# Output projection of an attention branch: plain fp32 operands in place of split halves, and a row broadcast written by ten copies in place of three

## The chip, the cores and the metric

The kernel runs on one core of a Trainium2 chip. The metric is the device time of one execution in microseconds (us). TensorE (PE in the profile) multiplies matrices, VectorE (DVE), ScalarE (ACT) and GpSimd (POOL) work elementwise, and SyncE (SP) issues nearly all transfers; these are carried by the core's 16 DMA engines. Each engine takes its instructions in the order in which they stand in its queue.

## The reference

Sequence length S = 2048, width D = 576, 32 heads of 18, a gate branch of width 2304. Cut to what matters:

```python
x = A_x
xn = layernorm(x)
qkv = (xn @ wqkv)                    # 32 heads, 18 wide
p = softmax(q k^T * 18**-0.5, masked to the last 256 positions)
s = (p @ v).reshape(1, S, D) @ wo    # the output projection
z1, z2 = split(gelu(xn @ w_in))      # 2304 each
g = silu((z1 * (w_sp @ layernorm(z2) + b_sp)) @ w_out)
return x + s * g
```

Everything is float32. The change concerns `s`: the division by the softmax's sums and the product with `wo`.

## The kernel before

**Precision by halves.** Most products are made from split operands. `split` (L117) writes a high part of a float32 tile in the type fp32r (a copy on ACT) and the rest, source minus high part, as a low part (a subtraction on DVE). A product is then three matmuls: high by high, high by low, low by high. Two places use plain fp32 operands: the products of probabilities with values (`pv`, L552, whose tiles `pt` and `vg` are fp32) and the transposes (L309). By its loops, `pv` issues 256 matmuls with 384 streamed columns, 224 with 256 and 224 with 128; four heads stand side by side in column groups of 32, so four such matmuls go together.

**The stages that the change touches.** They are the last three.

1. *The product stage* (L991 on) multiplies `w_sp` with the normed z2 by a Strassen scheme: three groups g of seven products n, with eight steps s each, so 168 steps m. One step is 18 matmuls (L1001) of 512 columns. For step m, `load_w` (L220, the DMA is on L224) brings the tile `spr` of 128 by 1024 four steps ahead into one of three buffers, so the load issued at step m waits for the split of the data of step m+1; `split_step` splits the data of step m+2 into `sph` (ACT, 1024 wide) and `spl` (DVE), both on L229. In the last group, idle room is used for what comes later. `pump` (L179) starts units from a list as credit allows and forms them two steps later; `later(k, ...)` (L917) puts a job k steps ahead.
2. *Units for the output projection.* `sums_unit` (L874), listed at step 124, loads the softmax's sums, inverts them, stores them as `r_d` (32 heads by 2048), and four steps later spreads them to `re_d`, one row for every row of the attention's output, by three copies from DRAM to DRAM: all 32 heads (576 rows), then two for the 64 rows that the layout repeats (10 rows of one head, 54 rows of three heads). A row is 2048 floats, 8,192 bytes. `weight_unit` (L854) loads and splits a block of `wo` or `w_out`, `o_unit` (L862) loads and divides the first two chunks of the output (`wo_load` L815, `wo_split` L826). `free_tile` (L896) reuses tiles of the products as they end: two tiles for the halves of `wo` (`wow`), four for ten blocks of `w_out` (`wos`).
3. *The bridge* (L1074 on) does the output projection for eight chunks t of 256 positions, two blocks of 128 each. A block is 14 pairs of stationary and streamed operand, each in two halves of 288 columns: 28 matmuls (L1100, `wops`). Beside them the next chunk is loaded, multiplied with the inverted sums and split, and four blocks of `w_out` and the first chunk of y are prepared. Its result goes through `so` (ACT L1114) to `s_d`.
4. *The end stage* multiplies y with `w_out`: 1728 matmuls of 288 columns (L1143, `po`), with the last four blocks of `w_out` loaded at its start.

The order of the queues is the program's own order there (a manual schedule for PE, ACT, DVE, POOL and SP in the product stage and the bridge, for PE in the end stage).

Of the kernel before, what the change touches and what calls it, by code (L numbers as in the profile page):

```python
# [9 lines left out]
F32 = mybir.dt.float32  # L10
F32R = mybir.dt.float32r
AF = mybir.ActivationFunctionType
ALU = mybir.AluOpType
# [45 lines left out]
def f32(ap):  # L59
    return ap.bitcast(F32)  # L60
# [3 lines left out]
def kernel(  # L64
# [52 lines left out]
    def split(hi, lo, src):  # L117
        act.activation(hi, src, AF.Copy)
        dve.tensor_tensor(lo, src, f32(hi), ALU.subtract)
# [695 lines left out]
    def wo_load(to, t, rooms):  # L815
        ts_ = slice(t * 2 * P, (t + 1) * 2 * P)
        raw = to.tile([P, 5, 2 * P], F32, name="oraw", bufs=1)
        rs = rooms()
        n = 5 // len(rs) + 1 if len(rs) > 1 else 5
        sp.dma_start(raw, o_d[:, ts_].rearrange("(k p) c -> p k c", p=P))  # L820
        for i, ap in enumerate(rs):
            kz = min(i * n + n, 5)
            sp.dma_start(ap[:, :kz - i * n], re_d[i * n * P:kz * P, ts_].rearrange("(k p) c -> p k c", p=P))
        return raw, rs

    def wo_split(ohl, got):  # L826
        raw, rs = got
        oh, ol = ohl[:, 0:5], ohl[:, 5:9]
        for n in range(3):
            ks = slice(2 * n, min(2 * n + 2, 5))  # L830
            rr = rs[0][:, ks] if len(rs) == 1 else rs[n][:, :ks.stop - ks.start]
            dve.tensor_tensor(raw[:, ks], raw[:, ks], rr, ALU.mult)
            act.activation(oh[:, ks], raw[:, ks], AF.Copy)
            if n < 2:
                dve.tensor_tensor(ol[:, ks], raw[:, ks], f32(oh[:, ks]), ALU.subtract)
            else:
                dve.tensor_tensor(oh[64:128, 4], raw[64:128, 4], f32(oh[64:128, 4]), ALU.subtract)
        return oh, ol

    wow, wos, parts, ohls = [], {}, [], {}  # L840

    with ExitStack() as ph:
        wk = open_pool(ph, "wk", bufs=2)
# [7 lines left out]
        OPENS = (0, 2, 4, 6)  # L851
        due, now = {}, 0

        def weight_unit(src, h, l):  # L854
            def load():
                raw = wk.tile([P, D], F32, name="zr", bufs=ZRB)
                sp.dma_start(raw, src)
                return raw

            return load, lambda raw: split(h, l, raw), 1  # L860

        def o_unit(t):  # L862
            def rooms():
                return [wk.tile([P, D], F32, name="zr", bufs=ZRB)[:, :512].rearrange("p (k c) -> p k c", k=2)
                        for _ in range(3)]

            def form(got):
                ohl = (pre.tile([P, 8 * ZW], F32R, name="z0")[:, :18 * P].rearrange("p (k c) -> p k c", k=9) if t else
                       ow.tile([P, 9, 2 * P], F32R, name="ohl", bufs=1))
                ohls[t] = wo_split(ohl, got)  # L870

            return lambda: wo_load(ow, t, rooms), form, 3

        def sums_unit():  # L874

            flat = [t.rearrange("h (a c) -> (h a) c", c=512) for t in (d_d, r_d)]

            def load():
                raw = wk.tile([P, D], F32, name="zr", bufs=ZRB)[:, :512]
                sp.dma_start(raw, flat[0])  # L880
                return raw

            def form(raw):
                dve.reciprocal(raw, raw)
                sp.dma_start(flat[1], raw)
                h, d = divmod(512, DH)
                for to, src in ((re_d[:D].rearrange("(h d) s -> h d s", d=DH),
                                 r_d.unsqueeze(1).to_broadcast([H, DH, S])),
                                (re_d[D:D + DH - d], r_d[h].unsqueeze(0).to_broadcast([DH - d, S])),
                                (re_d[D + DH - d:].rearrange("(h d) s -> h d s", d=DH),  # L890
                                 r_d[h + 1:].unsqueeze(1).to_broadcast([H - h - 1, DH, S]))):
                    later(4, sp.dma_start, to, src)

            return load, form, 1

        def free_tile(n):  # L896

            pool_, name = homes[PRODUCTS[n][1]]
            t = pool_.tile([P, 8 * ZW], F32R, name=name)
            made = [t[:, i * D:(i + 1) * D] for i in range(5)]  # L900
            if n < 3:
                wow.append(made)
                if n == 2:
                    return [weight_unit(wo[:, k, :], wow[0][k], wow[1][k]) for k in range(5)]
                return []
            parts.extend(made)
            us = [o_unit(n - 4)] if n in (4, 5) else []
            while len(parts) > 1:
                f = len(wos)
                wos[f] = parts.pop(0), parts.pop(0)  # L910
                us.append(weight_unit(w_out[f * P:(f + 1) * P, :], *wos[f]))
            return us
# [4 lines left out]
        def later(k, fn, *args):  # L917
            due.setdefault(now + k, []).append(partial(fn, *args))
# [109 lines left out]
    with ExitStack() as ph:  # L1028
# [22 lines left out]
        def wout_unit(to, f):  # L1051
            def load():
                raw = yp.tile([P, D], F32, name="wr")
                sp.dma_start(raw, w_out[f * P:(f + 1) * P, :])
                return raw

            def form(raw):
                split(*to, raw)
                wos[f] = to

            return load, form
# [12 lines left out]
        with ExitStack() as bridge:  # L1074
            zp = open_pool(bridge, "zp", bufs=2, side="right")
            wps = open_pool(bridge, "wps", bufs=2, space=PSUM)
            wl4 = yp.tile([P, 8 * D], F32R, name="wl4", bufs=1)

            def rooms():
                return [zp.tile([P, 5, 2 * P], F32, name="rraw")]  # L1080

            nxt = []
            ws = [wout_unit([wl4[:, (2 * n + a) * D:(2 * n + a + 1) * D] for a in range(2)], 10 + n) for n in range(4)]
            yu = [y_unit(0, k, nxt) for k in range(NF // 3)]
            plan = [ws[:2], ws[2:]] + [[y] for y in yu]
            oraws, got, outs = {}, [], []
            for t in range(NS // 2):
                if t + 2 < NS // 2:
                    oraws[t + 2] = wo_load((ow, zp)[t % 2], t + 2, rooms)
                oh, ol = ohls.pop(t)  # L1090
                for c in range(2):
                    cs = slice(c * P, (c + 1) * P)
                    po = wps.tile([P, 2, 512], F32, name="wops")
                    pl = []
                    for k in range(4):
                        pl += [(oh[:, k], wow[0][k]), (oh[:, k], wow[1][k]), (ol[:, k], wow[0][k])]
                    pl += [(oh[:, 4], wow[0][4]), (oh[:, 4], wow[1][4])]
                    for n, (lt, r) in enumerate(pl):
                        for i in range(2):
                            pe.matmul(po[:, i, :288], lt[:, cs], r[:, i * 288:(i + 1) * 288], start=n == 0,  # L1100
                                      stop=n == len(pl) - 1)
                    if c == 0:
                        if t and t + 1 < NS // 2:
                            to = (ow, zp)[(t + 1) % 2]
                            ohls[t + 1] = wo_split(to.tile([P, 9, 2 * P], F32R, name="ohl", bufs=1), oraws.pop(t + 1))
                    else:
                        while got:
                            form, raw = got.pop(0)
                            form(raw)
                        got = [(form, load()) for load, form in plan[t]]  # L1110
                    if outs:
                        sp.dma_start(*outs.pop(0))
                    so = zp.tile([P, D], F32, name="so")
                    act.activation(so.rearrange("p (a b) -> p a b", a=2), po[:, :, :288], AF.Copy)  # L1114
                    rows = slice(t * 2 * P + c * P, t * 2 * P + (c + 1) * P)
                    outs.append((s_d[rows, :], so))
            sp.dma_start(*outs.pop(0))
            while got:
                form, raw = got.pop(0)
                form(raw)  # L1120
# [3 lines left out]
        ph.enter_context(tc.manual_schedule(engines={ET.PE}))  # L1124
        outp = open_pool(ph, "outp", bufs=2, space=PSUM)
        fin = open_pool(ph, "fin", bufs=2)
        wow = [xp.tile([P, 8 * ZW], F32R, name=homes[PRODUCTS[n][1]][1]) for n in (1, 2)]
        more = [w[:, i * D:(i + 1) * D] for w in wow for i in range(4)]
        for f in range(14, NF):
            load_wout(more[2 * (f - 14):2 * (f - 14) + 2], f)  # L1130
        CH = list(range(8))
        for n, tc_ in enumerate(CH):
            ys = nxt
# [82 lines left out]
```

## Time and profile before

| what | value |
|---|---|
| median of 3 runs | 1939.07 us (1938.62 to 1939.74) |
| the profiled execution's own time | 1937.71 us |
| its span in the profile | 1936.0 us |
| PE busy | 1910.9 us, 99% of the span |
| DVE, ACT, POOL busy | 1076.2, 892.4, 288.1 us |
| matmuls of the output projection (L1100) | 448 |
| matmuls of the end stage (L1143) | 1728 |

The profile is one execution. A group's row names line, engine, operation, written and read tiles, shapes and count, then busy time, mean time of one, and idle time of the engine before them with what ended it. The chain of waits follows the work that ended last back to what released it. A row of a stage table gives for a stretch of time the busy time of each engine with its count, the granted PE clock, the mean busy share of the 16 DMA engines, and the GB/s that they moved. A matmul's recorded length includes its way through the array, so that records overlap: what one costs in a run is the distance from start to start.

### The profile page before, as it was taken

The numbers are of one execution on the slowest core, as the hardware profiler recorded it, in microseconds if no ns is written. First come the engines' busy times: TensorE is split into PE (matmuls) and PEld (weight loads), VectorE is DVE, ScalarE is ACT, GpSimd is POOL, SyncE is SP. The second block draws the span as 40 slices with busy tenths as digits, with TensorE's granted clock in tenths as the row PEclk, the third lists the DMA queues.
The fourth block names the chain that finished last, engine by engine and source line by source line (L and its number), as shares of the span: only waits on it lengthen the run. The fifth ranks groups of instructions, "written<-read, shape, count | busy, mean of one in ns | idle before, by whom it ended". The sixth has DMA issues, their size and how long they took to land.

```text
span 1936.0 us, 30625 instructions
## 1 busy us (share of the span) xinstructions
PE 1910.9 (99%) x11095; PEld 1658.4 (86%) x11095; DVE 1076.2 (56%) x2294; ACT 892.4 (46%) x1663; POOL 288.1 (15%) x388
## 2 busy tenths in 40 slices
PE   7999999999999999999999999999999999999998
PEld 5889999998777787877788888888888878999998
DVE  6522243367666666663277777666776877533322
ACT  4212222216665666666575566545655345422211
POOL 1101243433332333333100000000000000000000
PEclk9999999999999999999999999999999999999999
DMA  7655578975554655544576687757867778954442
GB/s 218 193 136 164 193 256 274 286 239 137 133 145 117 151 140 135 132 132 130 181 252 212 208 269 243 236 165 235 280 217 238 236 243 279 304 182 145 147 139 66
DMA packets 218510, 376.88 MB, mean 195 GB/s; under 512 B 40383, under 2 KB 117055, under 8 KB 217591
## 3 DMA queue, kind: packets, MB, share of 16 engines
q1 hardware_dynamic: 214135, 367.75, 61.9%
q10 hardware_dynamic: 2304, 5.09, 0.7%
q0 software_dynamic: 1920, 2.09, 0.4%
q8 instruction: 87, 1.43, 0.3%
q14 instruction: 64, 0.52, 0.1%
HBM read 261.76 MB, written 117.81 MB: 196 GB/s over the span
## 4 chain that ended last, share of the span: by engine, by line
PE 95%; DMA 3%; DVE 1%; ACT 1%; issue 0%; SPq 0%; DVEq 0%; ACTq 0%
PE acc L1001 34%; PE mm L460 12%; PE mm L688 12%; PE po L1143 12%; PE mm L326 6%; PE tps L539 5%; PE sp L409 5%; PE ops L562 4%; PE vps L478 3%; PE wops L1100 2%; DMA s_d<-so 1%; DMA spr<-sc_d 1%; DMA wraw<-in_wqkv_dram 1%; PE tpt L309 0%; DMA xr<-in_x_dram 0%
## 5 line engine op out<-in xcount | busy, mean ns | idle before, releaser
L1001 PE MATMUL acc<-sph,zh 128*128 128x512 f32 x1008 | 392.8, 390 | 3.8 <-ACT sph L229 3.7
L1001 PE MATMUL acc<-spl,zh 128*128 128x512 f32 x1008 | 393.0, 390 | 0.8 <-DVE spl L229 0.8
L1001 PE MATMUL acc<-sph,zl 128*128 128x512 f32 x1008 | 392.7, 390 | 0.0
L413 DVE CUSTOM_DVE_ANT_0 junk<-sp,band 128x384 bf16<-128x384 f32 (+1 forms) x512 | 273.7, 540 | 142.8 <-PE sp L409 138.6
L543 ACT ACTIVATE pt<-tps 128x384 f32<-128x384 f32 (+2 forms) x576 | 247.9, 439 | 125.4 <-PE tps L539 115.8
L460 PE MATMUL mm<-b,z1wh 128*128 128x512 f32 x648 | 250.2, 398 | 0.0
L229 DVE TENSOR_TENSOR spl<-spr,sph 128x1024 fp32r<-128x1024 f32 x166 | 203.2, 1224 | 65.7 <-ACT sph L229 64.8
L1001 PEld LDWEIGHTS acc<-sph,zh 128*128 128x128 f32 x1008 | 189.5, 188 | 44.1 <-ACT sph L229 4.1
L1001 PEld LDWEIGHTS acc<-spl,zh 128*128 128x128 f32 x1008 | 189.6, 188 | 40.7 <-DVE spl L229 1.1
L1001 PEld LDWEIGHTS acc<-sph,zl 128*128 128x128 f32 x1008 | 189.6, 188 | 39.2
L688 PE MATMUL mm<-z2wh,b 128*128 128x384 f32 x720 | 193.1, 335 | 0.0
L539 PE MATMUL tps<-att 128*128 128x384 f32 (+1 forms) x576 | 188.1, 327 | 0.9 <-ACT pt L543 0.8
L229 ACT ACTIVATE zh<-b 128x384 fp32r<-128x384 f32 x144 | 75.8, 527 | 241.2 <-PE acc L1001 241.1
L229 ACT ACTIVATE sph<-spr 128x1024 fp32r<-128x1024 f32 x166 | 174.2, 1049 | 20.2 <-DMA spr<-sc_d 10.4
L409 PE MATMUL sp<-att 118*128 118x384 f32 (+1 forms) x512 | 171.9, 336 | 0.0
L1143 PE MATMUL po<-b,yh 128*128 128x288 f32 x896 | 155.8, 296 | 0.0
L229 DVE TENSOR_TENSOR zl<-b,zh 128x384 fp32r<-128x384 f32 x144 | 80.1, 556 | 114.0 <-ACT zh L229 113.9
L460 PE MATMUL mm<-b,z1wl 128*128 128x512 f32 x360 | 142.7, 396 | 0.0
L460 PEld LDWEIGHTS mm<-b,z1wh 128*128 128x128 f32 x648 | 122.2, 189 | 23.9 <-issue 4.9
L688 PE MATMUL mm<-z2wl,b 128*128 128x384 f32 x400 | 134.0, 335 | 0.0
L539 PEld LDWEIGHTS tps<-att 128*128 128x128 f32 x576 | 109.1, 189 | 26.7 <-issue 7.6
L1143 PEld LDWEIGHTS po<-b,yh 128*128 128x128 f32 x896 | 131.9, 189 | 0.0
(159 smaller groups left out, 2793.9 us busy)
## 6 DMA issues: line engine op xcount, KB each, us to landing
spr<-sc_d SPq DMA_DIRECT2D x96, 512.0 KB
spr<-in_w_sp_dram SPq DMA_DIRECT2D x72, 512.0 KB
zr<-z_d SPq DMA_DIRECT2D x136, 192.0 KB
st_d<-qkhl SPq DMA_DIRECT2D x72, 256.0 KB
z_d<-zt SPq DMA_DIRECT2D x96, 192.0 KB
z_d<-z1o SPq DMA_DIRECT2D x72, 256.0 KB
z1t<-z_d SPq DMA_DIRECT2D x72, 256.0 KB
yr<-y_d SPq DMA_DIRECT2D x48, 384.0 KB
```

The source lines that it names most:

```text
L229: job()
L326: pe.matmul(ps, w, r, start=n == 0, stop=n == len(pl) - 1)
L409: pe.matmul(ps[:, :w], q_of(u, j)[:DR, i * P:(i + 1) * P], k_of(u, j)[:DR, k0:k0 + w], start=True, stop=True)
L413: dve.tensor_tensor_reduce(out=junk[:, :w], in0=ps[:, :w], in1=band[:, m0:m0 + w], scale=1.0, scalar=-3.0e38, op0=ALU.add, op1=ALU.max, ac ...
L460: pe.matmul(ps, w, r, start=n == 0, stop=n == len(pl) - 1)
L478: pe.matmul(ps[:, i, :288], r, w[:, i * 288:(i + 1) * 288], start=n == 0, stop=n == len(pl) - 1)
L539: pe.matmul(ps[:, :m * P], k_of(u, j)[:, (kb - base) * P:(kb - base + 1) * P], q_of(u, j)[:, (a - lo) * P:(a - lo + m) * P], start=True, s ...
L543: act.activation(pt[:, j, d0:d0 + n * P], ps[:, (qa - a) * P:(qa - a + n) * P], AF.Exp, scale=scale)
L562: pe.matmul(o_ps[c][32 * j:32 * j + 32, (lo - 4 * c) * P:(hi - 4 * c + 1) * P], vgs[u][:, kb - k0, j * VW:j * VW + 32], pt[:, j, (lo - kb) ...
L688: pe.matmul(ps[:, :ZW], r, wt, start=n == 0, stop=n == len(pl) - 1)
L1001: pe.matmul(acc[j], z[:, ps], w[:, cs], start=s == i == 0 and n in OPENS, stop=s == 7 and i == 2, skip_group_check=True)
L1143: pe.matmul(po[i][:, a, :288], y[:, i * P:(i + 1) * P], w[:, a * 288:(a + 1) * 288], start=f == 0 and m == 0, stop=f == NF - 1 and m == 2)
```

## The change

In words: `wo` is copied to one fp32 tile (ACT), not split. The divided output `o` is one fp32 tile, written by the DVE multiplication directly; its split (three copies on ACT, three subtractions on DVE a chunk) is gone. A block is five matmuls for each half of 288 columns, plain fp32, the fifth on 64 rows: 10 instead of 28. Only one product tile is needed for `wo`, so five tiles hold twelve blocks of `w_out`; the bridge then prepares blocks 12 to 15 and the end stage two instead of four. The spread of the inverted sums is ten copies, eight of four heads (72 rows) and the two for the repeated rows, two in a step over five steps.

```diff
-    def wo_split(ohl, got):
+    def wo_divide(o, got):
...
-            dve.tensor_tensor(raw[:, ks], raw[:, ks], rr, ALU.mult)
-            act.activation(oh[:, ks], raw[:, ks], AF.Copy)
...
+            dve.tensor_tensor(o[:, ks], raw[:, ks], rr, ALU.mult)
+        return o
...
-            return load, lambda raw: split(h, l, raw), 1
+            return load, lambda raw: split(h, l, raw) if l is not None else act.activation(h, raw, AF.Copy), 1
...
-                for to, src in ((re_d[:D].rearrange("(h d) s -> h d s", d=DH),
-                                 r_d.unsqueeze(1).to_broadcast([H, DH, S])),
-                                (re_d[D:D + DH - d], r_d[h].unsqueeze(0).to_broadcast([DH - d, S])),
-                                (re_d[D + DH - d:].rearrange("(h d) s -> h d s", d=DH),
-                                 r_d[h + 1:].unsqueeze(1).to_broadcast([H - h - 1, DH, S]))):
-                    later(4, sp.dma_start, to, src)
+                spread = [(re_d[h0 * DH:(h0 + 4) * DH].rearrange("(h d) s -> h d s", d=DH),
+                           r_d[h0:h0 + 4].unsqueeze(1).to_broadcast([4, DH, S])) for h0 in range(0, H, 4)]
+                spread += [(re_d[D:D + DH - d], r_d[h].unsqueeze(0).to_broadcast([DH - d, S])),
+                           (re_d[D + DH - d:].rearrange("(h d) s -> h d s", d=DH),
+                            r_d[h + 1:].unsqueeze(1).to_broadcast([H - h - 1, DH, S]))]
+                for n, (to, src) in enumerate(spread):
+                    later(4 + n // 2, lambda to=to, src=src: spreads.append(sp.dma_start(to, src)))
...
-                    pl = []
-                    for k in range(4):
-                        pl += [(oh[:, k], wow[0][k]), (oh[:, k], wow[1][k]), (ol[:, k], wow[0][k])]
-                    pl += [(oh[:, 4], wow[0][4]), (oh[:, 4], wow[1][4])]
-                    for n, (lt, r) in enumerate(pl):
+                    for k in range(5):
+                        kp = slice(0, P if k < 4 else 64)
                         for i in range(2):
-                            pe.matmul(po[:, i, :288], lt[:, cs], r[:, i * 288:(i + 1) * 288], start=n == 0,
-                                      stop=n == len(pl) - 1)
+                            pe.matmul(po[:, i, :288], o[kp, k, cs], wow[k][kp, i * 288:(i + 1) * 288], start=k == 0,
+                                      stop=k == 4)
```

How the queues stand, at the two places that matter most. First SP's queue in the last group of the product stage, where the inverted sums are spread (`re_d<-r_d`) between the loads of the product's tiles (`spr<-sc_d`), of blocks of `w_out` (`zr<-in_w_out_dram`) and of z1 (`z1t`). Before:

```order
L885 DMA r_d<-zr 128x512
L224 DMA spr<-sc_d 128x1024 x3
L857 DMA zr<-in_w_out_dram 128x576 x2
L224 DMA spr<-sc_d 128x1024
L1013 DMA re_d<-r_d 576x1x2048
L1013 DMA re_d<-r_d 10x2048
L1013 DMA re_d<-r_d 54x1x2048
L224 DMA spr<-sc_d 128x1024 x4
L929 DMA z1t<-z_d 128x512 x2
```

The same place of SP's queue in the change, from the load ahead of the first copy to the load behind the last:

```order
L224 DMA spr<-sc_d 128x1024
L852 DMA zr<-in_w_out_dram 128x576
L892 DMA re_d<-r_d 72x1x2048 x2
L224 DMA spr<-sc_d 128x1024
L852 DMA zr<-in_w_out_dram 128x576
L892 DMA re_d<-r_d 72x1x2048 x2
L224 DMA spr<-sc_d 128x1024
L892 DMA re_d<-r_d 72x1x2048 x2
L224 DMA spr<-sc_d 128x1024
L892 DMA re_d<-r_d 72x1x2048 x2
L224 DMA spr<-sc_d 128x1024
L892 DMA re_d<-r_d 10x2048
```

Behind these rows stand the copy of 54 rows, two loads of `z1t` and the next load of `spr`. The copies begin behind the same load as before, and each following load of `spr` now stands behind two more of them.

Second, PE's queue where the product stage ends and the bridge begins. Before, with the two halves of `wo` in turn (`b_15839`, `b_15840`) against the halves of the divided output (`ohl`):

```order
L1001 MATMUL acc_16766<-sph,zl 128x512
L1100 MATMUL wops<-b_15839,ohl 128x288 x2
L1100 MATMUL wops<-b_15840,ohl 128x288 x2
L1100 MATMUL wops<-b_15839,ohl 128x288 x4
L1100 MATMUL wops<-b_15840,ohl 128x288 x2
```

In the change, the whole bridge and the first matmuls of the end stage (`z_16801` is the divided output of the second chunk):

```order
L999 MATMUL acc_16770<-sph,zl 128x512
L1095 MATMUL wops<-b_15839,o 128x288 x20
L1095 MATMUL wops<-b_15839,z_16801 128x288 x20
L1095 MATMUL wops<-b_15839,o 128x288 x120
L1138 MATMUL po_17449<-b_15840,yh 128x288 x4
L1138 MATMUL po_17449<-b_15840,yl 128x288 x2
```

The bridge stands at the same place of PE's queue, with 160 matmuls where 448 were.

More of the change, by code (lines that the diff above doesn't have):

```diff
@@ L824, in wo_load @@
         return raw, rs
-    def wo_split(ohl, got):
+    def wo_divide(o, got):
         raw, rs = got
-        oh, ol = ohl[:, 0:5], ohl[:, 5:9]
         for n in range(3):
@@ L831, in wo_split @@
             rr = rs[0][:, ks] if len(rs) == 1 else rs[n][:, :ks.stop - ks.start]
-            dve.tensor_tensor(raw[:, ks], raw[:, ks], rr, ALU.mult)
-            act.activation(oh[:, ks], raw[:, ks], AF.Copy)
[L834 to L840, printed above, removed]
+            dve.tensor_tensor(o[:, ks], raw[:, ks], rr, ALU.mult)
+        return o
+    spreads = []
+    wow, wos, parts, divided = [], {}, [], {}
     with ExitStack() as ph:
@@ L852, with weight_unit @@
         due, now = {}, 0
-        def weight_unit(src, h, l):
+        def weight_unit(src, h, l=None):
             def load():
@@ L867, in form, with load @@
             def form(got):
[L868 to L872, printed above, removed]
+                o = (pre.tile([P, 8 * ZW], F32, name="z0")[:, :10 * P].rearrange("p (k c) -> p k c", k=5) if t else
+                     ow.tile([P, 5, 2 * P], F32, name="o", bufs=1))
+                divided[t] = wo_divide(o, got)
+            def load():
+                assert len(spreads) == 10
+                return wo_load(ow, t, rooms)
+            return load, form, 3
         def sums_unit():
@@ L898, in free_tile @@
             pool_, name = homes[PRODUCTS[n][1]]
-            t = pool_.tile([P, 8 * ZW], F32R, name=name)
+            t = pool_.tile([P, 8 * ZW], F32 if n == 1 else F32R, name=name)
             made = [t[:, i * D:(i + 1) * D] for i in range(5)]
[L901 to L905, printed above, removed]
+            if n == 1:
+                wow.extend(made)
+                return [weight_unit(wo[:, k, :], wow[k]) for k in range(5)]
             parts.extend(made)
@@ L1082 @@
             nxt = []
-            ws = [wout_unit([wl4[:, (2 * n + a) * D:(2 * n + a + 1) * D] for a in range(2)], 10 + n) for n in range(4)]
+            ws = [wout_unit([wl4[:, (2 * n + a) * D:(2 * n + a + 1) * D] for a in range(2)], 12 + n) for n in range(4)]
             yu = [y_unit(0, k, nxt) for k in range(NF // 3)]
@@ L1089 @@
                     oraws[t + 2] = wo_load((ow, zp)[t % 2], t + 2, rooms)
-                oh, ol = ohls.pop(t)
+                o = divided.pop(t)
                 for c in range(2):
@@ L1104 @@
                             to = (ow, zp)[(t + 1) % 2]
-                            ohls[t + 1] = wo_split(to.tile([P, 9, 2 * P], F32R, name="ohl", bufs=1), oraws.pop(t + 1))
+                            divided[t + 1] = wo_divide(to.tile([P, 5, 2 * P], F32, name="o", bufs=1), oraws.pop(t + 1))
                     else:
@@ L1126 @@
         fin = open_pool(ph, "fin", bufs=2)
-        wow = [xp.tile([P, 8 * ZW], F32R, name=homes[PRODUCTS[n][1]][1]) for n in (1, 2)]
+        wow = [xp.tile([P, 8 * ZW], F32R, name=homes[PRODUCTS[n][1]][1]) for n in (1,)]
         more = [w[:, i * D:(i + 1) * D] for w in wow for i in range(4)]
-        for f in range(14, NF):
-            load_wout(more[2 * (f - 14):2 * (f - 14) + 2], f)
+        for f in range(16, NF):
+            load_wout(more[2 * (f - 16):2 * (f - 16) + 2], f)
         CH = list(range(8))
```

## Prediction

> **What bounds the kernel now.** I read the page first, then a table by stages, then the chain of waits at the two places that the change touches.
>
> ```profile
> PE 1910.9 (99%) x11095; PEld 1658.4 (86%) x11095; DVE 1076.2 (56%) x2294; ACT 892.4 (46%) x1663; POOL 288.1 (15%) x388
> ```
>
> PE bounds the whole, so a change counts where it alters PE's work or makes PE wait. The table by stages (engines' busy time with counts, granted PE clock, DMA share, GB/s) for the spread of the sums, the bridge and the end stage:
>
> ```profile
> 1534.00:1560.00 26.00, 21.58 (x88) 17.20 (x87) 15.07 (x23) 8.99 (x13) 0.00 (x0) 0.93 0.76 268
> 1640.00:1701.00 61.00, 60.64 (x453) 60.17 (x452) 34.81 (x56) 25.28 (x44) 3.36 (x6) 1.00 0.83 277
> 1701.00:1936.00 235.00, 229.92 (x1725) 229.68 (x1723) 68.47 (x111) 50.54 (x80) 0.00 (x0) 1.00 0.43 135
> ```
>
> In the bridge PE is busy 60.64 of 61 us; DVE and ACT have half their time free. Only the first row shows idle PE: 26.00 less 21.58, 4.4 us, and a clock of 0.93, which loses 0.07 of 26 us, 1.8 us more. This stall costs 6.2 us. The chain of waits tells why, and gives the pace of the runs around it:
>
> ```profile
> 947.56 550.61 PE acc L1001 x2429
> ...
> 1534.03 20.28 DMA spr<-sc_d
> ...
> 1554.41 1.06 ACT sph L229
> ...
> 1555.50 1.24 DVE spl L229
> ...
> 1639.95 7.48 PE wops L1100 x56
> ...
> 1700.53 230.40 PE po L1143 x1728
> ```
>
> One load of `spr`, issued at 1534.03, took 20.28 us to land; ACT and DVE then split it and PE went on. SP's queue shows what stood ahead of it:
>
> ```profile
> 1529.95 0.33 SPq L224 DMA_DIRECT2D spr<-sc_d  x1
> 1530.32 2.27 SPq L1013 DMA_DIRECT2D re_d<-r_d  x3
> 1534.03 9.06 SPq L224 DMA_DIRECT2D spr<-sc_d  x3
> ```
>
> The three copies of the spread. So the change touches two things on PE's path: the bridge's matmuls and this stall.
>
> **The bridge's matmuls.** Removed: 448 split matmuls. 56 take 7.48 us, 134 ns each; from 1639.95 to the end stage at 1700.53 the bridge lasts 60.6 us. Added: 160 plain fp32 matmuls of the same 288 columns. The kernel has plain fp32 in two places. Records of `pv` (L562) and the run of one burst, then a run of fp32 transposes with the length of one:
>
> ```profile
> L562 PE MATMUL ops<-pt,vg 128*32 128x384 f32 x512 | 47.7, 491 | 0.0
> L562 PE MATMUL ops<-pt,vg 128*32 128x256 f32 x448 | 34.7, 381 | 0.0
> L562 PE MATMUL ops<-pt,vg 128*32 128x128 f32 x448 | 19.2, 274 | 0.0
> ...
> 488.96 2.80 PE L562 MATMUL ops<-pt,vg 128*32 128x384 f32 x48
> 491.69 0.50 PE L460 MATMUL mm<-b,z1wl 128*128 128x512 f32 x1
> ...
> 71.68 1.03 PE L309 MATMUL tpt<-ident,xr 128*128 128x128 f32 x8
> ...
> L309 PE MATMUL tpt<-ident,xr 128*128 128x128 f32 x7 | 0.9, 272 | 0.0
> ```
>
> The program issues 256, 224 and 224 matmuls in `pv`; the trace has 512, 448 and 448. A plain fp32 matmul is two records. What does a record cost? The burst's 48 records go four at a time on four column groups, so 12 sets in 2.73 us (488.96 to 491.69), 228 ns for 256 columns in the mean (the counts of the three widths are nearly equal), 0.89 ns a column. The eight transposes take 1.03 us; less the last one's 0.272 that is seven spacings of 108 ns for 128 columns, 0.85 ns a column, each with a full 128 by 128 weight, as in the bridge. The split matmul pays 134 ns for 288 columns, 0.46. So one record streams at half the split pace, and there are two. With the transposes' price (nearest in shape): 160 x 2 x 288 x 0.847 ns = 78.0 us; with the burst's 0.89: 82. The bridge goes from 60.6 to 78.0 us: **+17.4** (to +21). The fifth matmul on 64 rows streams the same columns and costs the same.
>
> What lies beside it: the DMA work in the bridge is 0.83 of 61 us, 51 us, under 78; the three ACT copies and three DVE subtractions that go were on engines with room, so they give nothing. The `w_out` blocks that move (two fewer at the end stage's start, two more in the product stage) are loads and splits beside PE; the end stage's 1728 matmuls take 230.40 us without a break and stay. All this I put at nothing; the cover is PE's own longer time.
>
> **The stall and the ten copies.** The same bytes are sent in smaller pieces, over five steps of 18 x 0.227 = 4.1 us. If pieces were all that mattered, the loads would slip between and the stall would go (a rival, below). But the DMA share of two stretches behind the issue says otherwise:
>
> ```profile
> 1534.00:1545.00 11.00, 11.00 (x50) 9.12 (x49) 10.57 (x17) 4.63 (x7) 0.00 (x0) 1.00 1.01 369
> 1553.00:1556.00 3.00, 0.48 (x1) 0.19 (x1) 0.50 (x1) 1.59 (x3) 0.00 (x0) 1.00 0.19 79
> ```
>
> Early all sixteen DMA engines work (share 1.01, 369 GB/s, 23.1 an engine). At the end the share is 0.19: three of sixteen, 79 GB/s, 26.3 an engine, while the load that PE waits for is not complete. Sixteen served the copy of 32 heads; three remain, and the last copy is the one of three heads. It has 54 rows, and 54 could be dealt to nine engines; it is the number of heads, the outer dimension of the source, that fits. A copy of four heads should then run on **four** engines. Are they the same four each time? The nearest rows are the stores of `o_d`, 18 rows each, four issued in a row:
>
> ```profile
> 596.61 1.65 SPq L588 DMA_DIRECT2D o_d<-ou  x4
> ...
> 598.35:599.15 0.80, 0.80 (x6) 0.71 (x5) 0.55 (x3) 0.64 (x2) 0.02 (x1) 1.00 0.52 159
> ```
>
> With several of them outstanding the share is 0.52, about eight or nine of sixteen (nine divides 18): they queue on one set, the rest idles. The Trainium skill, DMA: Bandwidth & Descriptors, section on why a DMA increments its semaphore by 16, states the rule: as many engines, at most 16, as divide the outermost dimension of both sides, and for such a queue always the lowest-numbered. No row names an engine; the shares agree with it, and by it all eight copies share engines 0 to 3.
>
> Check on today's stall: an engine of the three carries 36 rows of the big copy (294,912 bytes at 23.1 GB/s: 12.8 us), one of the ten (0.3), 18 of the 54 (147,456 at 26.3: 5.6), and its sixteenth of the 512 KB load (32,768 bytes: 1.25), 20.0 us together. The load landed at 1554.3, so the work began at 1534.3, 4 us behind the issue.
>
> The change, on the same engines: eight copies of 72 rows, 18 rows an engine, 5.6 us each: 44.8; the ten rows 0.3; the 54 rows 5.6; and by the queue's order five loads of `spr` up to the first one behind the last copy (6.2), one block of `w_out` (18,432 bytes, 0.7) and two loads of `z1t` (1.2). 58.8 us, so that fifth load lands at 1534.3 + 58.8 = 1593.1.
>
> When is it needed? PE ran dry before the late load at about 1551.7:
>
> ```profile
> 1551.47 0.39 PE L1001 MATMUL acc<-sph,zl 128*128 128x512 f32 x1
> 1555.52 0.50 PE L1001 MATMUL acc<-sph,zh 128*128 128x512 f32 x1 [3.67 <-ACT sph L229]
> ```
>
> Less ACT's 1.06, the first load was needed at 1550.6 and came 3.7 us late. The fifth is needed four steps (16.3 us) later, at 1566.9, and comes 26.2 late. What follows a landing (split, lower clock) is paid now too, so the stall grows by 26.2 - 3.7: **+22.5 us**. Bounds: if the copies begin at their issue, 4 us less (+18.5); at 23.1 GB/s an engine instead of 26.3, 58.8 becomes 67 (+31). Below +18.5 only another number of engines leads. The loads are issued in time: each waits for the split of three loads before. SP's later wait for the copies' end (the reads of `re_d`) falls when PE already stands.
>
> **Sum.** 17.4 + 22.5 = +39.9 us. On the profiled execution's 1937.71 that is 1977.6; on the median of 1939.07, 1.4 above it, **1979**. This case's own range, from the bounds: 1939.07 + 17.4 + 18.5 = 1975 to 1939.07 + 21 + 31 = 1991.
>
> **Rivals.**
>
> *The copies spread over all engines or over different sets* (0.10). For: the first copy of before uses sixteen, and smaller pieces let loads in between. Against: the 0.19 share at the end. Then two copies a step, 1.18 MB, with 0.52 of `spr` and 0.29 of `w_out`, 2.0 MB in 4.1 us against 369 GB/s x 4.1 = 1.5 MB, leave a backlog of 0.5 MB at each of three to four steps, under 6 us, and a load has 16 us. The stall's 6.2 goes: 1939.07 + 17.4 - 6.2 = 1950.
>
> *Faster: a plain matmul at full width costs what a split one does* (0.03), 134 ns, so that the bridge lasts 160 x 134 = 21.4 us, 39.2 less. It decides where the bridge falls under 60.6 - 22.5 = 38 us, 238 ns a matmul. For: matmuls fall from 28 to 10 a block. Against: the doubled records. With the longer stall: 1939.07 - 39.2 + 22.5 = 1922.
>
> *One record at half pace* (0.02): 160 x 244 ns = 39.0 us, 21.6 less, which the stall gives back: 1940. The Trainium skill, Perfetto Trace Analysis, section Engine Utilization, halves the array's rate for this fp32 mode, which would be this case; its page FP8 and Floating Point Precision, TensorE Precision Notes, counts four passes. The trace's two records at half pace are a quarter of the rate, and bear out the four.
>
> **Chances.** Forecast 0.83; sixteen engines 0.10; faster 0.03; half pace 0.02; 0.02 for anything else slower. 0.2%, about 4 us, is what a measurement of this kernel can tell from no change. Faster 0.03, same 0.02, slower 0.95. Forecast and sixteen engines lie on one side, with little between them; the range, 1968 to 1991, takes the forecast's own and 7 us below it, for an engine rate above today's 26.3, and leaves out the rest.
>
> **What would show it.** Right: 320 records on the bridge's line at about 244 ns a step, the bridge near 78 us; between 1534 and 1594 a DMA share near 4/16 with PE waiting for `sph` behind `spr` several times, in the product stage some 28 us idle and lost clock instead of 6. Wrong: a share near 1 while the copies run, or no PE wait there (the first rival); 160 records on the line, or a bridge under 45 us (the others); PE waiting for `o` or `so` in the bridge, a cost that I put at nothing.

## The result and the profile after

The change takes 1987.33 us in the median (1987.15 to 1987.78), the kernel before 1939.40: ratio 1.0248, interval 1.0230 to 1.0266, 48 us slower. The forecast was 1979 with a range of 1968 to 1991. Direction and both causes came as forecast; both terms of the sum were too small. Times below are medians of a kernel's runs; the stages are read from the one profiled execution of each.

PE's busy time grew, and it is still nearly the whole span. The page's row:

```profile
PE 1943.0 (98%) x10967; PEld 1661.5 (84%) x10967; DVE 1060.0 (53%) x2265; ACT 878.6 (44%) x1639; POOL 287.7 (14%) x388
```

The end of the chain of waits gives the stages, as it did before (bridge from 1639.95, end stage from 1700.53 for 230.40):

```profile
1659.93 6.13 PE acc L999 x27
1666.06 83.67 PE wops L1095 x320
1749.73 230.60 PE po L1138 x1728
```

The bridge begins 26.1 us later and lasts 83.7 us, 23.1 more; the end stage is the same. 26.1 + 23.1 + 0.2 is the whole difference of the spans (1985.4 - 1936.0 = 49.4). The three stages in the stage table, first the stretch of the spread:

```profile
1534.00:1600.00 66.00, 43.96 (x155) 33.47 (x154) 26.30 (x37) 19.18 (x29) 0.00 (x0) 0.83 0.52 187
1666.00:1750.00 84.00, 84.00 (x323) 58.17 (x322) 23.06 (x37) 15.88 (x25) 3.34 (x6) 1.00 0.61 204
1750.00:1985.00 235.00, 230.31 (x1728) 230.07 (x1726) 66.89 (x109) 49.68 (x79) 0.00 (x0) 1.00 0.41 131
```

In the bridge PE never waits. In the stretch of the spread it is idle 22 of 66 us, at a mean clock of 0.83. Taken as the prediction took the old stall (6.2 us), that is 22 + 0.17 x 66 = 33 us, where the forecast had some 28. PE's own rows in that stretch that were preceded by a wait, with its length and what ended it:

```profile
1561.58 0.80 PE L999 MATMUL acc<-sph,zh 128*128 128x512 f32 x1 [5.33 <-ACT sph L229]
...
1573.82 0.79 PE L999 MATMUL acc<-sph,zh 128*128 128x512 f32 x1 [4.43 <-ACT sph L229]
...
1586.08 0.79 PE L999 MATMUL acc<-sph,zh 128*128 128x512 f32 x1 [5.42 <-ACT sph L229]
...
1599.06 0.76 PE L999 MATMUL acc<-sph,zh 128*128 128x512 f32 x1 [5.46 <-DVE cb L953]
```

There are three long waits for `sph`, about 12.3 us apart, which is the time that two copies of four heads and one load need on four engines (2 x 5.6 + 1.25 = 12.5). ACT's rows show that the split itself waited for the load each time:

```profile
1560.47 1.06 ACT L229 ACTIVATE sph<-spr 128x1024 fp32r<-128x1024 f32 x1 [10.90 <-DMA spr<-sc_d]
...
1572.71 1.06 ACT L229 ACTIVATE sph<-spr 128x1024 fp32r<-128x1024 f32 x1 [10.19 <-DMA spr<-sc_d]
...
1584.97 1.06 ACT L229 ACTIVATE sph<-spr 128x1024 fp32r<-128x1024 f32 x1 [10.22 <-DMA spr<-sc_d]
```

And the DMA engines during the first of these waits:

```profile
1558.00:1562.00 4.00, 0.42 (x1) 0.29 (x1) 0.44 (x1) 1.53 (x2) 0.00 (x0) 0.89 0.25 107
```

A share of 0.25, four of sixteen, 107 GB/s or 26.7 an engine, while PE stands still: twelve engines have nothing to do.

The fourth wait is of another kind. A new product needs accumulators, and DVE has to empty them first (`cb`). In DVE's queue that work stands behind the splits of the next two loads:

```profile
1594.47 1.23 DVE L229 TENSOR_TENSOR spl<-spr,sph 128x1024 fp32r<-128x1024 f32 x1 [5.44 <-ACT sph L229]
1595.92 0.56 DVE L229 TENSOR_TENSOR zl<-b,zh 128x384 fp32r<-128x384 f32 x1 [0.23 <-ACT zh L229]
1597.09 1.22 DVE L229 TENSOR_TENSOR spl<-spr,sph 128x1024 fp32r<-128x1024 f32 x1 [0.60 <-ACT sph L229]
1598.23 3.67 DVE L953 TENSOR_TENSOR cb<-acc,t 128x512 f32<-128x512 f32 x6
```

The first of these splits is that of the load behind the last big copies. By the DMA completions in the trace that load landed at 1593.28, and ACT began on it at 1593.38.

### The profile page after: what moved, and what is told of

The parts are those of the page before. It is cut to its first block, busy times and chain, and to the rows that moved or that the text cites. A ratio compares the mean times of both kernels' runs of the same rounds, so it can differ in the third digit from the quotient of the medians.

```text
span 1985.4 us, 30320 instructions
## 1 busy us (share of the span) xinstructions
PE 1943.0 (98%) x10967; PEld 1661.5 (84%) x10967; DVE 1060.0 (53%) x2265; ACT 878.6 (44%) x1639; POOL 287.7 (14%) x388
## 4 chain that ended last, share of the span: by engine, by line
PE 95%; DMA 3%; DVE 1%; ACT 0%; issue 0%; SPq 0%; DVEq 0%; ACTq 0%
PE acc L999 33%; PE mm L460 12%; PE mm L688 12%; PE po L1138 12%; PE mm L326 6%; PE tps L539 5%; PE sp L409 5%; PE wops L1095 4%; PE ops L562 4%; PE vps L478 3%; DMA spr<-sc_d 2%; DMA re_d<-r_d 1%; PE tpt L309 0%; DMA xr<-in_x_dram 0%; ACT sph L229 0%
## 5 line engine op out<-in xcount | busy, mean ns | idle before, releaser
L999 PEld LDWEIGHTS acc<-sph,zh 128*128 128x128 f32 x1008 | 191.2, 190 | 62.9 <-ACT sph L229 16.4
L409 PE MATMUL sp<-att 118*128 118x384 f32 (+1 forms) x512 | 171.9, 336 | 0.0
```

The costliest lines, as they stand in the source:

```text
L409: pe.matmul(ps[:, :w], q_of(u, j)[:DR, i * P:(i + 1) * P], k_of(u, j)[:DR, k0:k0 + w], start=True, stop=True)
L999: pe.matmul(acc[j], z[:, ps], w[:, cs], start=s == i == 0 and n in OPENS, stop=s == 7 and i == 2, skip_group_check=True)
```

## The experiments

The runs test two theories for the product stage against each other, and two for the bridge. For the product stage, the theory of *the engines* says that a copy runs on as many DMA engines as divide its outer dimension, and that equal copies use the same ones. The theory of *the pieces* says that many copies between the loads hold these up, however they are dealt. For the bridge there is the forecast's price, two records at half pace, and, new from the trace of the change, the theory of *the rows*: going between weights of 128 and of 64 rows costs time. The change's start-to-start times in the bridge are 242 or 243 ns for 257 of the 319 steps; the other 62, four a block, are 332 to 347. In PE's queue of weight loads they stand where the rows change:

```profile
1669.87 0.78 PEld L1095 LDWEIGHTS wops<-b,o 64*128 64x128 f32 x4 [0.39 <-issue]
1671.03 0.30 PEld L1095 LDWEIGHTS wops<-b,o 128*128 128x128 f32 x2 [0.39 <-issue]
```

At each change of rows the weight loads stand idle for 0.39 us, where 0.05 is usual: the next weight is loaded as its matmul starts and not some 0.24 us ahead, and two matmuls start about 0.1 us late each.

The kernel before took 1938.31 us beside the first four runs and 1938.98 beside the rest. The product stage's length is from its first to its last matmul, 692.2 us before and 717.9 in the change.

**Dimensions swapped: nine engines a copy**

```diff
-(re_d[h0 * DH:(h0 + 4) * DH].rearrange("(h d) s -> h d s", d=DH), r_d[h0:h0 + 4].unsqueeze(1).to_broadcast([4, DH, S]))
+(re_d[h0 * DH:(h0 + 4) * DH].rearrange("(h d) s -> d h s", d=DH), r_d[h0:h0 + 4].unsqueeze(0).to_broadcast([DH, 4, S]))
...
-(re_d[D + DH - d:].rearrange("(h d) s -> h d s", d=DH), r_d[h + 1:].unsqueeze(1).to_broadcast([H - h - 1, DH, S]))
+(re_d[D + DH - d:].rearrange("(h d) s -> d h s", d=DH), r_d[h + 1:].unsqueeze(0).to_broadcast([DH, H - h - 1, S]))
```

> The changed kernel with one thing altered: in each of the eight copies, and in the one of three heads, the two outer dimensions are swapped (18 rows of a head outside, heads inside). Ten copies, their bytes, their row length of 8,192 bytes and their places in the queue stay. Theory of the engines (a copy runs on as many DMA engines as divide its outer dimension): nine engines a copy, 8 rows an engine, 2.5 us at 26.3 GB/s instead of 5.6; eight copies 20 us, the last 1.9, the loads between them 8, together 30 us instead of 59, so the fifth load lands near 1564, before it is needed at 1567. The product stage loses nothing there: of the 32.4 us that it loses in the changed kernel 31 to 32 go, and the time is 1955 to 1957. DMA share near 9/16 or more while the copies run. Rival, theory of the pieces (many DRAM to DRAM copies between the loads hold these up, however they are dealt to engines): no change, 1987, with the same waits.

1961.42 us, ratio 1.0114 (1.0099 to 1.0129): 23.1 us over its kernel before where the change is 47.9 over, so 25 us less by the order of two dimensions alone. The product stage takes 692.5 us. That is against the pieces. The long waits for `sph` are gone, and the share is well above a quarter, here while PE is busy:

```profile
1553.00:1557.00 4.00, 4.00 (x19) 3.33 (x18) 0.98 (x2) 0.75 (x1) 0.00 (x0) 1.00 0.81 298
```

But 4 to 6 us more than expected remain. PE's waits there:

```profile
1564.94 0.50 PE L999 MATMUL acc<-spl,zh 128*128 128x512 f32 x1 [0.66 <-DVE spl L229]
1573.08 0.47 PE L999 MATMUL acc<-sph,zh 128*128 128x512 f32 x1 [3.99 <-DVE cb L953]
```

The 3.99 is the change's fourth wait: the chain of waits leads from a load of `spr` that landed at 1567.32 over the splits to `cb`.

**The ten copies alone**

```diff
 (kernel before)
-later(4, sp.dma_start, to, src)            # three copies
+later(4 + n // 2, sp.dma_start, to, src)   # the change's ten
```

> The kernel before, with only its three copies replaced by the changed kernel's ten (four heads each); the output projection stays on split halves. If the two parts of the change simply add, the stall alone shows: 1939.4 + 25.8 (what the product stage takes longer in the trace of the change) = 1965. Theory of the engines: a share near 4/16 while PE waits. Rival: the longer product stage of the change is due to its other edits there (blocks of w_out that come earlier, wo not split), then this stays near 1940 or at 1933 without a stall.

1962.97 us, ratio 1.0126 (1.0109 to 1.0143), product stage 716.6 us: the copies alone make the long product stage, with the same three waits (13.4 us for `sph` in all) and the same fourth (5.2 for `cb`). The share while PE waits is not near 4/16 throughout, as was expected. Just before the first wait (1552 to 1556) it is 0.25 and in the third (1580 to 1582) 0.25 again, but in the first two us of the first wait it is 0.85: there the load issued at 1555.05 crosses the other engines.

**The projection alone**

```diff
 (the change)
-later(4 + n // 2, lambda to=to, src=src: spreads.append(sp.dma_start(to, src)))   # ten copies
+later(4, sp.dma_start, to, src)                                                   # three, as before
```

> The changed kernel with the three copies of before; the output projection on plain fp32 stays. Price of the projection alone: the bridge's 83.8 us in place of 60.6, so 1939.4 + 23.2 = 1962.6, with the old stall of 6 us. Rival: part of the bridge's 23 us comes from the late reads of the spread sums; then the bridge is shorter here, towards the predicted 78, and the time near 1957.

1961.99 us, ratio 1.0119 (1.0104 to 1.0134). The bridge is as long as in the change, so nothing of it came from the spread:

```profile
1641.84 83.67 PE wops L1093 x320
1725.51 74.58 PE po L1136 x558
```

The two parts add: 24.7 and 23.7 us over the kernel before in these runs, together 48.3, and the change was 47.9 over its own.

**The fifth matmul on 128 rows**

```diff
-return [weight_unit(wo[:, k, :], wow[k]) for k in range(5)]
+return [weight_unit(wo[:, k, :], wow[k], scale=1.0 if k < 4 else 0.5) for k in range(5)]
...
-kp = slice(0, P if k < 4 else 64)
+kp = slice(0, P)
```

> The changed kernel with the fifth matmul of each half on 128 rows in place of 64. The layout has those 64 rows twice, so the fifth block of wo is scaled by 0.5 as it is copied; the sum is the same. Theory of the rows: the four late starts a block (332 to 347 ns in place of 242, about 0.39 us a block in all) come with the change from weights of 128 rows to weights of 64 and back; they go, all steps in the bridge are 242 to 243, the bridge takes 77.6 us and the time is 1987.3 - 6.2 = 1981. Rival: they belong to the end of a block (another PSUM tile, the signal to ACT); then nothing changes, 1987.

1981.25 us, ratio 1.0217 (1.0202 to 1.0232), 6.1 under the change (5.0 with each taken against its own kernel before). Every start-to-start time is 242 or 243 ns, and the bridge is shorter by 6.1 us although the same columns stream:

```profile
1666.42 77.60 PE wops L1095 x320
1744.02 55.99 PE po L1138 x420
```

**Copies of two heads: the dose doubled**

```diff
-r_d[h0:h0 + 4].unsqueeze(1).to_broadcast([4, DH, S])) for h0 in range(0, H, 4)]
+r_d[h0:h0 + 2].unsqueeze(1).to_broadcast([2, DH, S])) for h0 in range(0, H, 2)]
...
-later(4 + n // 2, ...)
+later(4 + n // 4, ...)
```

> The changed kernel with the eight copies of four heads cut into sixteen of two heads (four in a step, the same five steps, the same bytes). Theory of the engines: the outer dimension is 2, so two engines carry all sixteen copies, 18 rows each, 5.6 us a copy as before, sixteen in a row: 89.7 us in place of 44.8 on those engines. The loads behind them come 45 us later: time 1987.3 + 45 = 2032 (2027 to 2040), DMA share near 2/16 while PE waits. Rival, theory of the pieces: twice as many, half as large pieces over the same steps let loads in earlier or cost a little more issue time; 1980 to 1995.

2032.35 us, ratio 1.0482 (1.0461 to 1.0503), as the theory of the engines had it. Smaller pieces made it 45 us worse. While the first of them run, before PE's buffers are used up, two of sixteen engines work:

```profile
1540.00:1550.00 10.00, 10.00 (x45) 8.26 (x45) 3.61 (x5) 2.13 (x4) 0.00 (x0) 1.00 0.12 52
```

From 1568 to 1580, where PE stands the whole time, the share is 0.13. The packets in the trace say the same more directly. Each row of a copy is one packet of 8,192 bytes, 640 in all; between the loads 4.0 engines at a time are busy with them in the change, 2.0 here, about 9 in the run with nine engines, and 16 while the run with copies of 16 heads (below) has one going.

**One record a matmul**

```diff
-t = pool_.tile([P, 8 * ZW], F32 if n == 1 else F32R, name=name)
+t = pool_.tile([P, 8 * ZW], F32R, name=name)
...
-ow.tile([P, 5, 2 * P], F32, name="o", bufs=1)
+ow.tile([P, 5, 2 * P], F32R, name="o", bufs=1)
```

(and so for the other two places where `o` is made)

> The changed kernel with the operands of the output projection in the type fp32r, nothing else: still five matmuls a half, but it leaves out the low halves, so the projection is computed at that type's reduced precision. If the price of plain fp32 is its two records at half pace, the trace has 160 records with 131 to 140 ns between starts and the bridge takes 160 x 134 = 21.4 us, up to 28 if the changes between 128 and 64 rows cost as much as in the change; then 1987.3 - 56 to 62 = 1925 to 1931. Rival: at so few matmuls the bridge is bound by loading, multiplying and evicting the chunks (the trace of the change has 0.61 x 84 = 51 us of DMA work in it); then the bridge takes about 50 us and the time is near 1954.

This kernel leaves out the low halves. 1955.08 us, ratio 1.0084 (1.0063 to 1.0104). The trace has 160 records in place of 320, so the type makes the second record. But the time went as the rival had it: the bridge lasts 52 us. Its stage row and PE's records of one kind:

```profile
1666.00:1717.00 51.00, 37.84 (x158) 30.65 (x157) 22.57 (x36) 15.70 (x24) 3.34 (x6) 0.68 0.96 328
...
L1095 PE MATMUL wops<-b,o 128*128 128x288 f32 x112 | 27.0, 405 | 13.2 <-ACT so L1109 13.2
```

The DMA engines are busy at 0.96, PE waits 13.2 us for `so`, whose tile is still being stored, and its clock falls to 0.68. So with these transfers the bridge has a floor of about 51 us, the DMA work that the prediction counted as hidden. Whether the 64 rows cost as much in this type can't be told here.

**The kernel before with a spread on sixteen engines**

```diff
 (kernel before)
+(re_d[h0 * DH:(h0 + 16) * DH].rearrange("(h d) s -> h d s", d=DH), r_d[h0:h0 + 16].unsqueeze(1).to_broadcast([16, DH, S]))   # h0 = 0, 16
+(re_d[D + DH - d:].rearrange("(h d) s -> d h s", d=DH), r_d[h + 1:].unsqueeze(0).to_broadcast([DH, H - h - 1, S]))
...
-later(4, sp.dma_start, to, src)
+later((4, 6, 8, 8)[n], sp.dma_start, to, src)
```

> The kernel before (projection on split halves) with another spread: two copies of 16 heads (sixteen engines, 18 rows an engine, 6.4 us each) two steps apart, and for the repeated rows the ten rows and the three heads with their dimensions swapped (nine engines), two steps later. Theory of the engines: no engine ever has more than about 8 us ahead of a load that has 16 us to come, so the stall of before goes: 1938.3 - 6.2 = 1932. Rival: as in the run with nine engines, a wait for the eviction behind a late split stays (4 us and the lower clock after it), because the loads of z1 and the reads of the spread sums meet there; then 1937 to 1939.

1932.19 us, ratio 0.9965 (0.9951 to 0.9979): the fastest of all, faster than both kernels. It writes the same bytes, and PE runs without a break where the kernel before and the change both stand:

```profile
1530.00:1560.00 30.00, 30.00 (x134) 24.86 (x133) 22.81 (x32) 12.75 (x18) 0.00 (x0) 1.00 0.95 352
```

The copies of 16 heads, their distance in the queue and the nine engines for the three heads came together here; none was run apart.

**The change with both causes taken away**

```diff
 (the change, with the spread of the run above and the fifth matmul on 128 rows)
```

> The changed kernel with both causes taken away: the spread of two copies of 16 heads (and nine engines for the three heads), and the fifth matmul on 128 rows (fifth block of wo scaled by 0.5). What stays is the price of plain fp32 alone, 77.4 us of bridge in place of 60.6: 1938.3 - 6.2 + 16.8 = 1949. Rival: the eviction's wait stays as in the run with nine engines; 1955.

1948.58 us, ratio 1.0050 (1.0035 to 1.0065). The bridge takes 77.6 us and the product stage has no long wait left (685.7 us). It is 16.4 us over the run before, which has the same spread, a product stage of the same 685.7 us, and the bridge on split halves (61.0 us): this is the price of plain fp32 itself.

## Why the prediction was right, point by point

- *The bridge, +17.4: right in kind, too small; +23.1.* Two records a matmul and 0.85 ns a column were right: 320 steps of 242 ns are 77.6 us, against 78.0. The step that failed is "The fifth matmul on 64 rows streams the same columns and costs the same." It streams the same columns, but the change to 64 rows and back costs 0.39 us a block, 6.1 us over 16 blocks. The run on 128 rows shows it alone. In the kernel before all 14 pairs had 128 rows, and it has no weights of 64 rows anywhere, so no row of it could show this. It does change between 118 and 128 rows (L409), and there nothing is lost: of 249 matmuls that follow one of 118 rows and 384 columns, nine in ten start 173 to 185 ns after it, 0.45 to 0.48 ns a column. So not every change of rows costs; the runs show the cost for 128 and 64 alone.
- *The stall, +22.5: right mechanism, a little small; +26.1* (1639.95 to 1666.06). Four engines, the same four, 26.3 GB/s each: the share of 0.25, the waits 12.3 us apart, nine engines (25 us less) and two engines (45 us more) bear each part out. The fifth load was counted to land at 1593.1 and landed at 1593.28. The last tenths of that are luck: the start of 1534.3 was inferred from the kernel before, where the copies' first packet is at 1532.52, and happens to fit the change, where it is at 1534.08. The term that was mis-sized is "What follows a landing (split, lower clock) is paid now too". After the last late landing PE pays more than the old stall did: it has reached the end of a product, DVE empties the accumulators only behind two late splits, and PE goes on at 1599.06. That is 5.8 us behind the landing, where the kernel before took 1.2 (1554.31 to 1555.52); these 4.6 us are more than the 3.6 by which the stall's term was short. This fourth wait is read from the chain and came back with nine engines (3.99); no run took it away alone.
- *The loads issued in time: not quite.* SP itself stood in the issue of loads and copies, as below. The stall came out near the count all the same, since the engines were the longer chain.
- *What was put at nothing stayed at nothing:* the end stage (230.60 against 230.40), the moved `w_out` blocks (the product stage takes 685.7 us with them and without, in the last two runs), ACT and DVE in the bridge, where PE never waits.
- *The rivals.* Sixteen engines: not the change, but its price was near: 6.2 us, where the run on the kernel before gained 6.8. The two rivals with one record were wrong in more than their record: with one record a matmul, in fp32r, the bridge still lasted 52 us, where they had 21.4 and 39.0.

## What to carry to other kernels

The shape of a transfer decides how many DMA engines carry it: look at the DMA share while something waits, and where it is a small fraction of sixteen with a wait behind it, change the order or the size of the outer dimension before cutting a transfer into pieces. Price a plain fp32 matmul of this shape (288 columns) as two records at half pace, 484 ns or about 3.6 of the split kind, so that it pays only where it replaces four or more; here it replaced 2.8. Where the last weights of a run have 64 rows and the others 128, try padding or scaling them to 128.

## What the runs showed that was not expected

SP can stand in the issue of a transfer. The median issue takes 0.36 us; behind the copies on four engines one took up to 8.84, and four copies of two heads took 18.09 together. In the change, then with copies of two heads:

```profile
1546.26 3.73 SPq L224 DMA_DIRECT2D spr<-sc_d  x1
1550.03 2.75 SPq L892 DMA_DIRECT2D re_d<-r_d  x2
1553.72 8.84 SPq L224 DMA_DIRECT2D spr<-sc_d  x1
```

```profile
1536.42 18.09 SPq L892 DMA_DIRECT2D re_d<-r_d  x4
1554.60 4.29 SPq L224 DMA_DIRECT2D spr<-sc_d  x1
```

In all the traces an issue of over 3 us stands only among the copies of four or two heads and right behind them, with their long backlog on few engines; that the backlog causes it was not tested apart. And a change of weight rows between 128 and 64 costs about 0.2 us each way, by the two late starts that follow it (about 335 and 347 ns in place of 242).
